# TensorE instead of VectorE for the transposes of couples 6 to 11, with natural rows, in an attention-plus-SiLU kernel

## The chip, the cores and the metric

The kernel runs on one core of a Trainium2 chip. The metric is the device time of one execution in microseconds (us). The engines are named as in the profile: PE (TensorE, matmuls), PEld (its weight loads), DVE (VectorE), ACT (ScalarE), POOL (GpSimd), SP (SyncE, which here only issues DMAs).

## The reference

Inputs: q, k, v of shape (8 batches, 12 heads, 448 tokens, 64), gains g_q and g_k of 64, w_in (768 x 2048), w_out (2048 x 768), all float32. Cut to what is computed:

```python
q_n = q / sqrt(mean(q*q, -1) + 1e-6) * g_q          # k_n likewise with g_k
scores = (1/8) * q_n @ k_n.T                        # per batch and head
attn = exp(scores - max); attn /= sum(attn) + 1e-9
x = (attn @ v)  -> (8*448, 12*64) = (3584, 768)     # heads side by side
h = x @ w_in
out = (h * sigmoid(h)) @ w_out                      # (3584, 768)
```

## The kernel before, in words

**Units of work.** A *couple* is two pairs of heads, that is four heads of one batch; a batch has three couples and the kernel NC = 24, counted here from 0. `GROUP` is 6: six couples are two batches. The outer loop is `for c in range(NC): visit(c); between(c)`. `visit(c)` is the attention of couple c: `scores` (L701, PE, with the exponentials in L706 on ACT) and `weigh` (L738, PE, the product with v) take turns, and `divide` (L796, DVE) multiplies the result of couple c-1 with the reciprocal row sums and puts it into xT. `between(c)` prepares couple c+1 and the norms of c+2, and runs the *filler*.

**The filler.** From couple 4 on, matmuls of the first dense layer for batches that are done stand between the visits. They come from a generator (`halves_in`, with `Seven`: a Strassen-Winograd scheme with seven products of three matmul steps, L870) that `fill(others, prompt)` steps on for a given number of columns. `others` are small pieces of work dealt out evenly over these steps; `prompt` are pieces dealt at the first step and then every third. Each product is written into one of two PSUM banks "mm", and taken out by ACT (L878, L888) or DVE (L828); POOL adds two intermediate sums (L890, L891). A finished block gets silu on ACT (L1008) and is stored to a DRAM tensor `hidden` by SP (`save`, L903) from one of three `stage` buffers, which is free for the next block when the store has landed. After the last couple, the second dense layer runs in seven quads (L1177, L1214), from 743 us to the end, and stores the output.

**Weights.** Pieces of w_in are fetched (L84), taken apart and rounded on ACT, DVE and POOL (L99, L100, L122 to L133) among the fill pieces until couple 9 or so, and their Strassen sums are formed on DVE (L825, L828).

**Norms and transposes.** Scores need q and k with the head dimension on the partitions. The root mean square of k is not applied to k: it is the scale of the exponentials (`norm.column`). That of q is multiplied into the rows of q by POOL. There are two ways:

- *Early way, couples 0 to 5.* Rows of q and k are loaded in natural rows of 256 bytes or more: 112 partitions with four neighbouring tokens each for q, 128 partitions with three each for k. `norm.squares_q` and `squares_k` square on ACT (L458) and reduce on DVE (L459); `norm.root` makes mean plus epsilon on DVE (L483) and the power -0.5 on POOL (L487); `norm.scale` multiplies q on POOL (L502). `transpose_q` (L620) and `transpose_k` (L636) transpose on PE against the identity `ident` into a PSUM tile "sc" (two buffers, shared with the scores), and ACT copies qT (L624) and kT with the gains (L638) out.
- *Late way, couples 6 to 23.* q is loaded in eight pieces of 128-byte runs (`load_quarters`, L249), k twice: plain, in six DMAs, for the norms (L276, L278), and in eight quarters for the transposes. `flip` transposes 32 x 32 blocks of q and of k on DVE (L644, L647), and `gain` multiplies kT with the gains on ACT (L653). The squares of q (`sum_squares`: L661 on ACT, L662 on DVE) then lie in halves on two partitions, so `scale(c)` adds them with two matmuls against `ident` (L673), after `pair_up` has changed `ident` for that (L686); the root follows on DVE (L674) and POOL (L677), the multiplication on POOL (L680). v comes in four DMAs (L303) and four for the rest (L314, L316), against one (L307) and three (L320, L323) in the early way.

Tokens of couples 0 to 5 (batches 0 and 1) thus lie permuted (token 4p + j at column 112 j + p), and `store` undoes this when it writes the output, in pieces that are cut at 112 rows. From batch 2 on (`plain=2`) the order is natural and pieces are cut at the end of a batch only.

**Order.** The order on each engine is the order in which the program issues, written out by hand. SP takes its DMAs in program order too, and waits at each for what it needs: a load that waits for a buffer holds up all that is behind it. In `between(c)` of the late way the order is: `flip` q of c+1 and the load of q for c+2 behind it; a first fill, with the key norms of c+2 among its others; `sum_up` (row sums of couple c, L772); a second fill, with the two halves of the reciprocals (L781, the second followed by `spread`, which moves them between partitions by six DMAs, L787 and L789), `flip` of k, `gain` and `sum_squares(c+2)` as prompt pieces; then `scale(c+2)`. For c = 5 the same pieces run without a fill between them, and the norms of couple 6 stand in visit 5.

Of the kernel before, what the change touches and what calls it, by code (L numbers as in the profile page):

```python
# [30 lines left out]
class Shapes:  # L31
    def __init__(self, q, w_in):
# [19 lines left out]
        assert self.NW == self.NPAIR and self.B % 2 == 0  # L52

        self.Q = 32
        assert 2 * self.S == self.NK and 4 * self.Q == self.P and self.D == 2 * self.Q
# [134 lines left out]
def kernel(  # L190
# [25 lines left out]
    nc = tc.nc  # L216
# [34 lines left out]
    def load_q(c, t, steps=1):  # L251


        b, cp = divmod(c, z.NPAIR // 2)
        rows = q[b, ts(cp, 4)]
        if c >= z.NPAIR:
            load_quarters(rows, t)
            return
        for i in range(steps):
            n = 4 // steps  # L260
            dst = t[0:R, ts(i, nq // steps)].rearrange("p (n j d) -> p n (j d)", n=n, j=J)
            nc.sync.dma_start(dst, rows[ts(i, n)].rearrange("n (p j) d -> p n (j d)", j=J))
# [5 lines left out]
    def load_k(c):  # L268
        t = place[f"k{c % 2}"]
        if c >= z.NPAIR:  # L270
            t = place["k0"]
            for i, start in enumerate((z.KA, z.KB)):
                main, left = plain(k, c, i)
                dst = t[:, ds(start, z.KL)].rearrange("p (j h d) -> p h j d", j=z.KEYS, h=2)
                for h in range(2):
                    nc.sync.dma_start(dst[:, h], main[:, h])  # L276
                dst = t[ds(i * z.LEFT, z.LEFT), ds(z.KL, 2 * D)]
                nc.sync.dma_start(dst.rearrange("p (h d) -> p h d", h=2), left)  # L278
            return
# [17 lines left out]
    def load_v(c):  # L297
        if c >= z.NPAIR:
            dst = place["v"].rearrange("p (i h j d) -> p i h j d", i=2, h=2, d=D)
# [9 lines left out]
    def load_v_rest(c):  # L309
        if c >= z.NPAIR:  # L310
            for i in range(2):
# [215 lines left out]
def bounded(  # L527
# [12 lines left out]
    )  # L540
    GROUP = z.NPAIR
    EARLY = GROUP - 1

# [67 lines left out]
    def transpose_q(c):  # L611
# [13 lines left out]
        if c == GROUP - 2:  # L625
            load_q(GROUP)

    def transpose_k(c):
# [9 lines left out]
        nc.scalar.activation(kT, columns, AF.Copy, scale=gains)  # L638
        loads["k" if c < GROUP - 1 else "quarters"](min(c + 2, GROUP))

# [159 lines left out]
    def normalise(c):  # L800


        def piece(name, i):
            if name == "q":
                norm.squares_q(c, raw_of(c), scratch[i], i)
                norm.root(c, name, i)
                norm.scale(c, raw_of(c), q_of(c), i, nc.gpsimd)
                if i == 1 and c + 2 < GROUP:
                    load_q(c + 2)
            else:  # L810
                late = c >= GROUP
                rows = place["k0" if late else f"k{c % 2}"]
                norm.squares_k(c, rows, scratch[0 if late else i], i)
                if i == 1:
                    norm.root(c, name)
                    if late and c + 1 < NC:
                        loads["k"](c + 1)

# [401 lines left out]
    def save_out(q, i, j):  # L1220
        for t in range(2):
            store(
                nc, out, z, (4 * q + 2 * (i - 1) + t) * P, results[i, j][t], (j - 1) * z.HALF,
                nc.gpsimd if q == QUADS - 1 and i == 2 else nc.sync, plain=2,
            )

    def quad(q):
# [53 lines left out]
        if q == QUADS - 1:  # L1281

            def then(t, h):
                store(
                    nc, out, z, (4 * q + t) * P, c[1, 2][t][:, ts(h, QUARTER)],
                    z.HALF + h * QUARTER, *((nc.scalar, nc.sync)[:: 1 if h else -1]), plain=2,
                )
# [75 lines left out]
    def visit(c):  # L1363

        if c < GROUP - 1:
            beside = normalise(c + 1)
        elif c == GROUP - 1:
            beside = [lambda: sum_squares(c + 1), lambda: scale(c + 1)] + normalise(c + 1)[2:]
        else:
            beside = []  # L1370
        if c < NC:
            scores(c, 0, 0)
        run_all(beside[0:1])
        if c > 0:
            weigh(c - 1, LEFT)
            weigh(c - 1, LEFT - 1, 0)
            turn(1, nc.scalar.copy if c < GROUP else nc.vector.tensor_copy)
        if c < NC:
# [47 lines left out]
    def between(c):  # L1426

        def transposes_and_sums():
            summing = sum_up(c)
            if c < GROUP:  # L1430
                next(summing)
            if c < GROUP - 1:
                transpose_k(c + 1)
            reciprocals = next(summing)
            if GROUP - 1 <= c < NC - 1:
                reciprocals += [lambda: flip(c + 1, "k"), gain]
# [3 lines left out]

        if c < GROUP - 1:
            transpose_q(c + 1)
# [272 lines left out]
```

## Time and profile before

| | us |
|---|---|
| median of three runs (1344.6 to 1344.99) | 1344.6 |
| the profiled execution, its own time | 1346.0 |
| its span, first to last instruction | 1344.1 |
| PE busy | 1300.4 |
| DVE busy | 951.8 |
| ACT busy | 502.3 |
| POOL busy | 369.5 |

The granted clock of PE over the span is 0.994 of full speed. "Busy" is the union of the instructions' times. A row of an instruction group reads: line, engine, operation, what is written and read, shapes, count, then busy time, the mean of one in ns, and the idle time of the engine just before them with what ended it. A row of the time order reads: start, duration, engine, line, operation, and in brackets the idle time before it and its releaser. Windows of the span are given in us from its start.

### The profile page before, as it was taken

What the parts mean: (1) busy time and instruction counts of PE and PEld (TensorE: products, weight loads), DVE (VectorE), ACT (ScalarE), POOL (GpSimd) and SP (SyncE); (2) the same over time, 40 slices, a digit from 0 to 9 for tenths busy, and PEclk for the clock granted to TensorE, in tenths of its full rate; (3) what the DMA queues carried; (4) which work ended last, traced back from release to release, by engine and by line L of the source; (5) the groups of instructions that cost most, each with busy time, mean ns of one, the idle gap of its engine ahead of it and who ended that gap; (6) DMA issues with size and microseconds to landing.
All of it is one profiled execution on the core that took longest, in us unless ns stands there. A gap on an engine that the chain in (4) does not pass through costs nothing.

```text
span 1344.1 us, 19812 instructions
## 1 busy us (share of the span) xinstructions
PE 1300.4 (97%) x7111; PEld 828.3 (62%) x7111; DVE 951.8 (71%) x1630; ACT 502.3 (37%) x877; POOL 369.5 (27%) x223
## 2 busy tenths in 40 slices
PE   8997998999999999999999999999999999999997
PEld 4332443444444444444444455557999999999997
DVE  5786876785855655855554586789978787878785
ACT  7874455556445545455544244420000000101000
POOL 5765344443343343343331044410000000000000
PEclk9998999999999999999999999999999999999999
DMA  8565456434433543443421257422323232332311
GB/s 230 155 147 123 119 155 161 106 89 109 108 91 88 124 93 87 124 97 86 112 74 38 101 176 262 149 98 71 103 75 99 75 102 77 99 100 79 125 48 39
DMA packets 286543, 147.69 MB, mean 110 GB/s; under 512 B 224420, under 2 KB 270372, under 8 KB 286436
## 3 DMA queue, kind: packets, MB, share of 16 engines
q1 hardware_dynamic: 285872, 145.35, 39.6%
q8 instruction: 58, 0.95, 0.3%
q0 software_dynamic: 256, 0.79, 0.2%
q14 instruction: 49, 0.40, 0.1%
q10 hardware_dynamic: 308, 0.20, 0.0%
HBM read 96.73 MB, written 41.29 MB: 103 GB/s over the span
## 4 chain that ended last, share of the span: by engine, by line
PE 81%; DVE 7%; ACT 4%; DMA 3%; issue 2%; SPq 2%; POOL 0%; ACTq 0%; DVEq 0%
PE mm L870 24%; PE alone L1177 22%; PE av L738 8%; PE sc L701 8%; PE mm L1177 7%; PE alone L870 7%; PE alone L1214 2%; DVE work L781 1%; DVE work L752 1%; DMA rows<-in_k_dram 1%; PE sc L772 1%; SPq L249 1%; DVE sums_x L825 1%; PE mm L1214 1%; ACT L1008 1%
## 5 line engine op out<-in xcount | busy, mean ns | idle before, releaser
L870 PE MATMUL mm<-x,W 128*128 128x448 f32 x636 | 258.6, 549 | 12.0 <-DVE parts L828 3.3
L706 ACT ACTIVATE work<-sc,rms 128x448 f32<-128x448 f32 x324 | 185.5, 635 | 86.2 <-PE sc L701 62.8
L870 PEld LDWEIGHTS mm<-x,W 128*128 128x128 f32 x636 | 117.6, 191 | 146.8 <-issue 114.7
L870 PE MATMUL mm<-sums_x,W 128*128 128x448 f32 x456 | 186.5, 548 | 6.8 <-DVE parts L828 4.8
L701 PE MATMUL sc<-work 64*64 64x448 f32 x1344 | 167.3, 550 | 1.7 <-DVE rms L674 1.1
L738 PE MATMUL av<-work,rows 64*64 64x448 f32 x1296 | 156.0, 546 | 4.7 <-ACT av L714 1.8
L752 DVE TENSOR_TENSOR work<-work 128x896 f32<-128x896 f32 (+1 forms) x114 | 123.7, 1115 | 49.4 <-PE av L738 48.8
L870 PEld LDWEIGHTS mm<-sums_x,W 128*128 128x128 f32 x456 | 85.1, 191 | 100.2 <-issue 83.4
L487 POOL TENSOR_TENSOR rms<-rms,minus_half 128x14 f32<-128x14 f32 (+3 forms) x37 | 88.3, 2389 | 134.6 <-DVE rms L483 133.9
L514 POOL DMA_DIRECT2D out_dram<-x x2 | 1.3, 652 | 443.0 <-DVE x L828 443.0
L1177 PE MATMUL alone<-W,rows 128*128 128x192 f32 x608 | 113.0, 326 | 0.0
L738 PEld LDWEIGHTS av<-work,rows 64*64 64x64 f32 x1296 | 60.7, 133 | 76.0 <-issue 35.4
L677 POOL TENSOR_TENSOR rms<-rms,minus_half 128x28 f32<-128x28 f32 x18 | 86.2, 4791 | 74.7 <-DVE rms L674 63.3
L1177 PEld LDWEIGHTS alone<-W,rows 128*128 128x128 f32 x608 | 101.2, 190 | 0.0
L701 PEld LDWEIGHTS sc<-work 64*64 64x64 f32 x1344 | 55.5, 134 | 69.1 <-ACT work L706 26.9
L890 POOL TENSOR_TENSOR parts<-parts,stage 128x448 f32<-128x448 f32 x31 | 42.0, 1355 | 150.3 <-DVE parts L828 149.9
L1177 PE MATMUL alone<-W,work 128*128 128x192 f32 x382 | 72.2, 326 | 0.0
L1008 ACT ACTIVATE stage<-stage 128x896 f32<-128x896 f32 x63 | 57.4, 947 | 24.7 <-DVE stage L828 24.1
L1177 PEld LDWEIGHTS alone<-W,work 128*128 128x128 f32 x382 | 63.8, 190 | 0.0
L1187 ACT COPY rows<-alone 128x192 f32<-128x192 f32 x34 | 10.9, 320 | 137.4 <-PE alone L1177 78.9
L781 DVE RECIPROCAL work<-sc 128x224 f32<-128x224 f32 x36 | 55.6, 1547 | 5.2 <-PE sc L772 5.0
L459 DVE TENSOR_REDUCE rms<-rows 128x8 f32<-128x512 f32 (+2 forms) x48 | 30.2, 629 | 40.3 <-ACT rows L458 37.5
(243 smaller groups left out, 2104.9 us busy)
## 6 DMA issues: line engine op xcount, KB each, us to landing
hidden<-stage SPq DMA_DIRECT2D x63, 448.0 KB, 3.1
work<-hidden SPq DMA_DIRECT2D x21, 1024.0 KB, 5.1
rows<-in_moe_w_out_dram SPq DMA_DIRECT2D x32, 384.0 KB, 3.4
W<-in_moe_w_in_dram SPq DMA_DIRECT2D x22, 512.0 KB, 5.0
work<-work SPq DMA_DIRECT2D x144, 56.0 KB, 2.0
rows<-in_q_dram SPq DMA_DIRECT2D x144, 56.0 KB, 2.3
rows<-in_k_dram SPq DMA_DIRECT2D x144, 56.0 KB, 2.4
x<-hidden SPq DMA_DIRECT2D x7, 1024.0 KB, 5.6
```

The costliest lines, as they stand in the source:

```text
L487: nc.gpsimd.tensor_tensor(out=t, in0=t, in1=half, op=ALU.pow)
L677: nc.gpsimd.tensor_tensor(out=f, in0=f, in1=minus_half.to_broadcast([P, n]), op=ALU.pow)
L701: nc.tensor.matmul(two[ds(half * D, D), h, 0:S], keys[rows, ts(half, D)], qT[rows, pair, :], start=True, stop=True,)
L706: nc.scalar.activation(eleft[:, h] if j == LEFT else weights(c, j)[:, i, h], two[:, h, 0:S], AF.Exp, scale=norm.column(c, i, h, j),)
L738: nc.tensor.matmul(sums[i][ds(h * D, D), :], v, w, start=(j == 0 and step == 1), stop=(j == LEFT - 1 and step == 1),)
L752: nc.vector.tensor_tensor(out=total, in0=total, in1=more, op=ALU.add)
L781: nc.vector.reciprocal(out=r[0][:, rows], in_=t[:, rows])
L870: nc.tensor.matmul(t, self.left(name, s), self.right(name, s), start=s == ends[0], stop=s == ends[1])
L890: nc.gpsimd.tensor_tensor(out=u2, in0=u2, in1=p5, op=ALU.add)
L1008: nc.scalar.activation(t, t, AF.Silu)
L1177: nc.tensor.matmul(t, x[:, i], y, start=i == ORDER[0], stop=i == ORDER[-1])
L1214: nc.tensor.matmul(o, a[:, 2 * i + m, t], right_one(name, i)[:, m], start=n == 0, stop=n == len(steps) - 1,)
```

## The change

A constant `LATE` = 12 takes the place of `GROUP` = 6 as the couple from which the late way is used. Couples 6 to 11 go the early way for loads, norms and transposes, with these differences from couples 0 to 5: q is loaded by two DMAs straight into the place where it is scaled, in the order j, h, d (256-byte runs); one root serves both halves of q, followed by two scales in place; the norms of q for couple c+2 are dealt as others of the second fill (for couples 6 and 7 they stand in visits 5 and 6). `pair_up`, the first `sum_squares` and the first `scale` of the late way move to `between(10)`. Tokens of batches 2 and 3 are permuted too, so the output of four batches is stored in the cut pieces (`plain=4`).

```diff
+        self.LATE = 2 * self.NPAIR
 def load_q(c, t, steps=1):
+        if c >= z.LATE:
+            load_quarters(rows, t)
+            return
         if c >= z.NPAIR:
-            load_quarters(rows, t)
+            for i in range(2):
+                dst = t[0:R, ts(i, nq // 2)].rearrange("p (j h d) -> p j h d", j=J, h=2)
+                nc.sync.dma_start(dst, rows[ts(i, 2)].rearrange("h (p j) d -> p j h d", j=J))
             return
 def load_k(c):  # the same in load_v and load_v_rest
-        if c >= z.NPAIR:
+        if c >= z.LATE:
 def transpose_q(c):
         if c == GROUP - 2:
             load_q(GROUP)
+        elif c >= GROUP:
+            load_q(c + 1)
 def transpose_k(c):
-        loads["k" if c < GROUP - 1 else "quarters"](min(c + 2, GROUP))
+        loads["k" if c < LATE - 1 else "quarters"](min(c + 2, LATE))
 def normalise(c):
         def piece(name, i):
+            t = scratch[i if c < GROUP + 2 else 0]
+            source = raw_of(c) if c < GROUP else q_of(c)
             if name == "q":
-                norm.squares_q(c, raw_of(c), scratch[i], i)
+                norm.squares_q(c, source, t, i)
+            else:
+                norm.squares_k(c, place["k0" if c >= LATE else f"k{c % 2}"], t, i)
+            if name == "q" and c < GROUP:
                 norm.root(c, name, i)
-                norm.scale(c, raw_of(c), q_of(c), i, nc.gpsimd)
+                norm.scale(c, source, q_of(c), i, nc.gpsimd)
...
+            elif i == 1:
+                norm.root(c, name)
+                if name == "q":
+                    for m in range(2):
+                        norm.scale(c, source, q_of(c), m, nc.gpsimd)
+                elif LATE <= c < NC - 1:
+                    loads["k"](c + 1)
 def save_out(q, i, j):  # and in the last quad
-                nc.gpsimd if q == QUADS - 1 and i == 2 else nc.sync, plain=2,
+                nc.gpsimd if q == QUADS - 1 and i == 2 else nc.sync, plain=4,
 def visit(c):
-        if c < GROUP - 1:
-            beside = normalise(c + 1)
-        elif c == GROUP - 1:
-            beside = [lambda: sum_squares(c + 1), lambda: scale(c + 1)] + normalise(c + 1)[2:]
-        else:
-            beside = []
+        beside = normalise(c + 1) if c <= GROUP else []
 def between(c):
-            if c < GROUP - 1:
+            if c < LATE - 1:
                 transpose_k(c + 1)
             reciprocals = next(summing)
-            if GROUP - 1 <= c < NC - 1:
+            if LATE - 1 <= c < NC - 1:
                 reciprocals += [lambda: flip(c + 1, "k"), gain]
...
-        if c < GROUP - 1:
+        if c < LATE - 1:
             transpose_q(c + 1)
         elif c < NC - 1:
             flip(c + 1, "q")
...
-        further = normalise(c + 2)[2:] if c >= GROUP - 1 else []
-        queries = [lambda: sum_squares(c + 2)] if c >= GROUP - 1 else []
-        fill(late + weights_in(c, 0) + further)
+        further = normalise(c + 2) if c >= GROUP - 1 else []
+        fill(late + weights_in(c, 0) + further[2:])
...
-        fill(weights_in(c, 1), prompt[:3] + [lambda: run_all(prompt[3:] + queries)])
-        if c == GROUP - 2:
-            pair_up()
+        if c >= LATE - 2:
+            if c == LATE - 2:
+                prompt.append(pair_up)
+            queries = prompt[3:] + [lambda: sum_squares(c + 2)]
+            fill(weights_in(c, 1), prompt[:3] + [lambda: run_all(queries)])
+        else:
+            fill(weights_in(c, 1) + (further[:2] if c >= GROUP else []), prompt)
...
-        if c >= GROUP - 1:
+        if c >= LATE - 2:
             scale(c + 2)
```

More of the change, by code (lines that the diff above doesn't have):

```diff
@@ L297, in load_v @@
     def load_v(c):
-        if c >= z.NPAIR:
+        if c >= z.LATE:
             dst = place["v"].rearrange("p (i h j d) -> p i h j d", i=2, h=2, d=D)
@@ L309, in load_v_rest @@
     def load_v_rest(c):
-        if c >= z.NPAIR:
+        if c >= z.LATE:
             for i in range(2):
@@ L540, in bounded @@
     )
-    GROUP = z.NPAIR
+    GROUP, LATE = z.NPAIR, z.LATE
     EARLY = GROUP - 1
@@ L803, in piece @@
         def piece(name, i):
+            t = scratch[i if c < GROUP + 2 else 0]
+            source = raw_of(c) if c < GROUP else q_of(c)
             if name == "q":
-                norm.squares_q(c, raw_of(c), scratch[i], i)
+                norm.squares_q(c, source, t, i)
+            else:
+                norm.squares_k(c, place["k0" if c >= LATE else f"k{c % 2}"], t, i)
+            if name == "q" and c < GROUP:
                 norm.root(c, name, i)
-                norm.scale(c, raw_of(c), q_of(c), i, nc.gpsimd)
+                norm.scale(c, source, q_of(c), i, nc.gpsimd)
                 if i == 1 and c + 2 < GROUP:
                     load_q(c + 2)
-            else:
[L811 to L817, printed above, removed]
+            elif i == 1:
[5 more added lines that the diff above has]
+                    loads["k"](c + 1)
         if c >= NC:
@@ L1285, in then @@
                     nc, out, z, (4 * q + t) * P, c[1, 2][t][:, ts(h, QUARTER)],
-                    z.HALF + h * QUARTER, *((nc.scalar, nc.sync)[:: 1 if h else -1]), plain=2,
+                    z.HALF + h * QUARTER, *((nc.scalar, nc.sync)[:: 1 if h else -1]), plain=4,
                 )
@@ L1363, in visit @@
     def visit(c):
-        if c < GROUP - 1:
-            beside = normalise(c + 1)
-        elif c == GROUP - 1:
-            beside = [lambda: sum_squares(c + 1), lambda: scale(c + 1)] + normalise(c + 1)[2:]
-        else:
-            beside = []
+        beside = normalise(c + 1) if c <= GROUP else []
         if c < NC:
@@ L1376, in visit @@
             weigh(c - 1, LEFT - 1, 0)
-            turn(1, nc.scalar.copy if c < GROUP else nc.vector.tensor_copy)
+            turn(1, nc.scalar.copy if c <= GROUP else nc.vector.tensor_copy)
         if c < NC:
```

## The prediction, made before the changed kernel was run

> **What bounds the kernel now.** I read the page's busy shares first, then cut the span into couples (a couple's visit begins with its first scores matmul, L701) with the table by stage, then read the order of time in the couples that the change touches.
>
> ```profile
> PE 1300.4 (97%) x7111; PEld 828.3 (62%) x7111; DVE 951.8 (71%) x1630; ACT 502.3 (37%) x877; POOL 369.5 (27%) x223
> ...
> 103.40:131.40 28.00, 21.26 (x153) 7.68 (x152) 19.53 (x26) 15.42 (x28) 16.08 (x10) 0.90 0.50 108
> 131.40:168.90 37.50, 35.04 (x179) 15.60 (x178) 30.06 (x45) 17.91 (x29) 15.28 (x9) 0.93 0.49 118
> 168.90:203.40 34.50, 32.90 (x178) 14.89 (x177) 26.71 (x36) 20.09 (x33) 16.60 (x9) 1.00 0.60 152
> 203.40:243.40 40.00, 34.40 (x175) 15.63 (x174) 27.17 (x35) 20.53 (x34) 16.71 (x9) 0.96 0.55 144
> 243.40:276.80 33.40, 32.59 (x175) 15.02 (x174) 27.96 (x35) 20.21 (x33) 15.20 (x8) 1.00 0.44 105
> 276.80:313.10 36.30, 32.79 (x176) 15.10 (x176) 29.34 (x35) 18.95 (x31) 16.45 (x8) 1.00 0.44 111
> ```
>
> The first line is the whole kernel: PE bounds it. The rest are couples 5 to 10 (counted from 0), one line each: window, its length, busy time of PE, PEld, DVE, ACT and POOL, then granted clock. Length less PE busy is PE's idle time: 6.7, 2.5, 1.6, 5.6, 0.8 and 3.5 us. Couples 13 to 21, which do the same with VectorE's transposes but without the rounding of w_in, have at most 0.4 us each. So just the couples where the change works leave PE 14 us idle (6 to 10), after 6.7 in couple 5, and only they run at a granted clock below 1. Two places carry it. The end of couple 5, in order of time (start, duration, engine, line; in brackets the idle time before and who ended it):
>
> ```profile
> 122.76 4.12 PE L870 MATMUL mm<-x,W 128*128 128x448 f32 x6 [2.38 <-DVE work L781]
> 130.80 0.62 PE L673 MATMUL sc<-rms,ident 128*128 128x28 f32 x2 [3.92 <-DVE rms L662]
> 131.36 1.77 PE L701 MATMUL sc<-work 64*64 64x448 f32 x8
> ...
> 168.85 0.98 PE L701 MATMUL sc<-work 64*64 64x448 f32 x8
> ```
>
> PE waits 2.4 us for the reciprocals (L781), then about 4 us for the sums of squares of couple 7's queries (L662); the eight matmuls after it take 1.77 us instead of 0.98, which is the halved clock. And couple 8:
>
> ```profile
> 219.65 2.31 SPq L303 DMA_DIRECT2D rows<-in_v_dram  x4
> 222.05 4.07 SPq L249 DMA_DIRECT2D rows<-in_q_dram  x8
> 226.22 0.90 SPq L903 DMA_DIRECT2D hidden<-stage  x2
> 229.50 0.53 ACT L888 COPY stage<-mm 128x448 f32<-128x448 f32 x1 [8.56 <-DMA hidden<-stage]
> 230.08 2.52 PE L870 MATMUL mm<-x,W 128*128 128x448 f32 x6 [2.55 <-ACT stage L888]
> 234.62 4.22 PE L870 MATMUL mm<-sums_x,W 128*128 128x448 f32 x6 [2.02 <-DVE parts L828]
> ```
>
> The silu rows were ready at 219.8, but their save stands on SP behind four v loads and eight q loads; the stage buffer comes free at 229.5, ACT sits 8.6 us, PE runs out of banks twice, and the clock drops again (0.96).
>
> [...] slow matmuls run from 122.8 to 126 and from about 130 to 136 us, after 2.4 and 3.9 us of idling. [...] the trace has 273 ns (L636) and 259 ns (L620), but groups of eight pass in 0.8 to 0.9 us because they overlap, and couples 1 to 4, which use them, keep a clock of 1.00. [...] one subtraction of L825 took 1.73 us beside the scale on POOL (L680), 0.62 otherwise.
>
> **The change part by part.** Prices are the rows of before:
>
> ```profile
> L677 POOL TENSOR_TENSOR rms<-rms,minus_half 128x28 f32<-128x28 f32 x18 | 86.2, 4791 | 74.7 <-DVE rms L674 63.3 <-DVE av L714 9.3 <-DMA rows<-in_k_dram 2.2
> L680 POOL TENSOR_TENSOR rows<-rows,rms 128x896 f32<-128x896 f32 x18 | 32.3, 1796 | 1.4
> L644 DVE STREAM_TRANSPOSE work<-rows 128x896 f32<-128x896 f32 x18 | 19.8, 1102 | 0.0
> L662 DVE TENSOR_REDUCE rms<-rows 128x28 f32<-128x896 f32 x18 | 19.5, 1086 | 22.8 <-ACT rows L661 21.6 <-ACT av L714 1.1
> L624 ACT COPY work<-sc 128x896 f32<-128x896 f32 x5 | 4.5, 908 | 0.0
> ```
>
> 1. *PE, added, on the path.* Eight q and seven k transposes for each of couples 6 to 11, in couples 5 to 10. In couples 3 and 4 the q group held PE 0.82 and 0.92 us (73.30 to 74.22, 93.52 to 94.34), the k group 0.91. About 1.78 us, six times: **+10.7**. The k group's wait for its score bank (0.46 and 0.73 us there) stays out: it now follows a whole fill. Nor does the q group idle there.
> 2. *PE, removed.* Six pairs of L673 at 0.30: **-1.8**. The waits before them: about 4.1 in couple 5 (28.00 less 21.26 less the 2.4 for L781) and 0.5 in couple 9: **-4.6**. What is late next: couple 6's first scores need only the copied qT and kT and the key roots, all done by about 119; divide of couple 5 needs the spread of the reciprocals, and SP issues that at once instead of after eight q loads (119.2 to 124.0). The 2.4 us for L781 stays: the bank is held by the same two reciprocals.
> 3. *Clock.* Couples 5 and 6 lose 0.10 x 28 + 0.07 x 37.5 = 5.4 us. The second stretch, some 6.8 us at half speed, follows the L673 wait and goes: **-3.4**. The first stays. Bounds: 0 to -5.4.
> 4. *SP.* A couple's loads fall from 30 DMAs (q 8, k 6 + 8, v 4 + 4) to 10 (2, 4, 1 + 3). At 0.48 us (median of L249) to 0.6 that is about 9 us of queue less per couple. In couple 8, from 217.1 on, v's rest, v and q take about 3.6 us instead of 9: the save is issued near 221, its buffer is free near 224, before PE wanted the bank (227.5). Of 5.6 us idle I keep 0.8: **-4.8**, and its clock loss, 0.04 x 40: **-1.6**. Bounds: 0 to -7.2.
> 5. *DVE.* Per couple -1.10 - 1.07 (the block transposes) - 1.09 - 0.19, + two reduces at 0.68 + 0.35: -1.7 us. It pays only where PE waits for DVE: couples 7 and 10: **-0.6** and **-1.2**, bounds 0 and -5. Couple 6 gets it the other way: the squares of couple 7 now stand in visit 6 ahead of the twelve operations of sum_x, which end just when the fill begins (145.9 against 144.8): 0.9 us of DVE, and its scale then blocks sum_x: **+1.0**, bounds -2 to +2.5. That scale ends some 0.5 us before the transposes of q 7 want it; if late, PE waits, and behind it the whole fill.
> 6. *ACT*: one copy of 0.91 and 0.3 of squares more per couple; gain (1.04) becomes the copy of kT. It ran 20 of 34 us, so 0; without that cover 0.9 us ahead of an eviction in each of six couples. In return ACT no longer sits in gain waiting for the key flip (4.7 and 5.1 us in couples 7 and 8), with evictions behind it.
> 7. *POOL*: 4.79 + 1.70 go; a root of 16 columns comes (2.58 for 14, 4.79 for 28: about 2.9) and two scales at 1.04. Less by 1.5, at the fill's end or in the visit, where no L890 waits: 0.
> 8. *Moved to couples 10 and 11*: the pairing of ident (four copies at 0.2 us on POOL), 16 quarter loads and the first L673; couples 13 to 21 show these hidden in steady state: 0, at worst +1.
> 9. *Stores.* Batches 2 and 3 are cut at 112 rows too: six more pieces in each column half, 12 DMAs on an SP that mostly waits for results: 0.
>
> Sum: 10.7 - 1.8 - 4.6 - 3.4 - 4.8 - 1.6 - 0.6 - 1.2 + 1.0 = **-6.3** against the profiled run's 1346.0 (span 1344.1 and 1.9 around it). The median of the runs is 1.4 lower, 1344.6, so the forecast is 1338.3.
>
> **The rivals.** *More gain*: no clock drop at all (another 2 us) and DVE's relief takes most idle time of couples 6, 7 and 10: -12, 1332.6. For it: all those waits name DVE. Against: PE then meets ACT and the reciprocals. *Wash*: the 2.4 us wait still triggers the clock drop for its full length (+2 to 3.4) and couple 8 is half cured (+3): about -0.5, 1344.1. *Slower*, by one mechanism: idle time re-forms behind the transposes. PE pays 10.7 and saves 6.4 certainly; if the save of couple 8 is still late (SP stands until 216.5 behind a w_in load that waits for POOL, whatever the other loads cost) and the clock falls as before, nothing else comes back, and couple 6 adds its 1.0: +5.3, 1349.9. It decides once ACT's wait at L888 in couple 8 stays over about 6 us. Against it: of the queue after 217.1, two thirds are loads that go. The diff leaves no room for the change not doing what it says.
>
> **How the numbers follow.** Chances: forecast 0.60, more gain 0.17, wash 0.14, slower 0.09. 0.2% is 2.7 us, about what a measurement of this kernel can tell from no change. Faster takes the first two whole but for 0.03, and 0.04 of the wash: 0.78; within, 0.13; slower, 0.09. The range goes from the larger gain to just past the wash: 1332 to 1346.
>
> **What would show it.** Right: no L673 before couple 10, a clock of 1 in couple 8, no ACT wait of over 3 us on hidden<-stage, couples 5 to 10 together 209.7 - 6 = some 203 us, couples from 12 on as before. Wrong: PE idle over 2 us in couple 8, a clock under 0.93 in couples 5 or 6, or the transposes waiting for POOL.

## The result and the profile after

The changed kernel takes **1333.36 us** (median of 6 runs, 1331.46 to 1335.99) against 1344.2 (6 runs, 1342.48 to 1344.99): ratio 0.9921, 95% interval 0.9908 to 0.9935. That is 10.8 us less, where 6.3 less was forecast. The profiled execution took 1333.6 us. The diff adds lines, so L701 is now L709, L738 L746, L870 L882, L673 L681, L781 L789, L828 L840, L888 L900, L878 L890 and L903 L915.

The first view is the page, busy time by engine; the next the table by stage with the same columns as before (window, length, busy time of PE, PEld, DVE, ACT and POOL, granted clock), one line for each of couples 5 to 10.

```profile
PE 1301.7 (98%) x7189; PEld 833.1 (63%) x7189; DVE 942.2 (71%) x1623; ACT 506.6 (38%) x890; POOL 363.8 (27%) x229
```

```profile
103.40:123.60 20.20, 19.24 (x164) 7.77 (x163) 14.12 (x19) 14.80 (x29) 10.99 (x5) 1.00 0.40 98
123.60:162.20 38.60, 36.08 (x190) 16.65 (x189) 32.71 (x51) 21.55 (x36) 19.28 (x12) 0.96 0.39 105
162.20:196.40 34.20, 33.58 (x188) 16.34 (x188) 24.31 (x34) 19.97 (x35) 14.55 (x10) 1.00 0.46 135
196.40:231.50 35.10, 34.00 (x189) 16.17 (x189) 24.88 (x35) 21.14 (x35) 15.79 (x10) 1.00 0.55 152
231.50:264.80 33.30, 33.30 (x188) 16.41 (x187) 24.91 (x32) 21.21 (x36) 13.30 (x8) 1.00 0.34 94
264.80:301.50 36.70, 34.56 (x194) 15.54 (x193) 29.62 (x35) 19.76 (x31) 17.33 (x13) 1.00 0.41 106
```

PE is as busy as before, with 78 more instructions, while the span fell from 1344.1 to 1331.8. The six couples take 198.1 us together instead of 209.7, which is 11.6 of the 12.3; the work after the last couple takes 600.5 instead of 601.1, so the cut stores cost nothing. Couple 5 is 7.8 us shorter, couple 8 is 5.0 shorter, and of these six only couple 6 has a clock below 1.

The end of couple 5 in order of time:

```profile
119.63 2.97 DVE L789 RECIPROCAL work<-mm 128x224 f32<-128x224 f32 x2 [2.16 <-PE mm L780]
120.53 0.53 ACT L890 COPY stage<-mm 128x448 f32<-128x448 f32 x1 [1.58 <-PE mm L882]
121.11 2.52 PE L882 MATMUL mm<-x,W 128*128 128x448 f32 x6 [0.62 <-ACT stage L890]
123.56 0.98 PE L709 MATMUL sc<-work 64*64 64x448 f32 x8
```

There is no L681 and no 4 us wait any more, and the 2.38 us for the reciprocals are gone too: PE waits 0.62 us for an eviction by ACT (a copy that takes a product out of its bank), and the first scores of couple 6 follow at full speed. The reciprocals themselves (L789) run until 122.60, but the fill's last product starts at 121.11: it does not wait for their bank, as there are two. Couple 8, in order of time:

```profile
205.33 3.50 SPq L85 DMA_DIRECT2D W<-in_moe_w_in_dram  x2
...
211.27 0.54 SPq L313 DMA_DIRECT2D rows<-in_v_dram  x1
211.92 1.91 SPq L263 DMA_DIRECT2D rows<-in_q_dram  x2
213.92 1.62 SPq L915 DMA_DIRECT2D hidden<-stage  x2
...
219.00 0.53 ACT L900 COPY stage<-mm 128x448 f32<-128x448 f32 x1 [4.31 <-PE sc L644]
```

One v DMA and two q DMAs stand where four and eight stood. ACT's eviction L900 now ends its idle time on PE's own transposes (L644), not on the landing of `hidden`, and couple 8 keeps a clock of 1.00.

### The profile page after: what moved, and what is told of

It is laid out like the page before. It is cut to its first block, busy times and chain, and to the rows that moved or that the text cites. A ratio compares the mean times of both kernels' runs of the same rounds, so it can differ in the third digit from the quotient of the medians.

```text
span 1331.8 us, 19793 instructions
## 1 busy us (share of the span) xinstructions
PE 1301.7 (98%) x7189; PEld 833.1 (63%) x7189; DVE 942.2 (71%) x1623; ACT 506.6 (38%) x890; POOL 363.8 (27%) x229
## 4 chain that ended last, share of the span: by engine, by line
PE 84%; DVE 7%; ACT 3%; issue 3%; DMA 2%; POOL 1%; SPq 0%; ACTq 0%; DVEq 0%; POOLq 0%
PE mm L882 26%; PE alone L1189 22%; PE av L746 8%; PE sc L709 7%; PE mm L1189 7%; PE alone L882 7%; PE alone L1226 2%; DVE work L760 1%; PE sc L780 1%; DVE work L789 1%; DVE sums_x L837 1%; DMA work<-work 1%; PE mm L1226 1%; PE sc L644 1%; PE sc L626 0%
## 5 line engine op out<-in xcount | busy, mean ns | idle before, releaser
L882 PE MATMUL mm<-x,W 128*128 128x448 f32 x636 | 256.7, 546 | 6.1 <-DVE parts L840 2.3
L714 ACT ACTIVATE work<-sc,rms 128x448 f32<-128x448 f32 x324 | 184.7, 633 | 81.0 <-PE sc L709 64.9
L882 PEld LDWEIGHTS mm<-x,W 128*128 128x128 f32 x636 | 116.7, 190 | 138.0 <-issue 109.0
L882 PE MATMUL mm<-sums_x,W 128*128 128x448 f32 x456 | 183.7, 543 | 1.6 <-DVE parts L840 1.6
L709 PE MATMUL sc<-work 64*64 64x448 f32 x1344 | 168.2, 549 | 2.6 <-ACT work L714 1.4
L746 PE MATMUL av<-work,rows 64*64 64x448 f32 x1296 | 156.6, 543 | 6.3 <-ACT av L722 1.8
L493 POOL TENSOR_TENSOR rms<-rms,minus_half 128x14 f32<-128x14 f32 (+4 forms) x43 | 106.4, 2476 | 149.8 <-DVE rms L489 140.2
L882 PEld LDWEIGHTS mm<-sums_x,W 128*128 128x128 f32 x456 | 85.1, 190 | 90.7 <-issue 82.8
L746 PEld LDWEIGHTS av<-work,rows 64*64 64x64 f32 x1296 | 59.9, 133 | 78.0 <-issue 35.5
L709 PEld LDWEIGHTS sc<-work 64*64 64x64 f32 x1344 | 55.2, 134 | 73.8 <-ACT work L714 27.6
L685 POOL TENSOR_TENSOR rms<-rms,minus_half 128x28 f32<-128x28 f32 x12 | 57.5, 4794 | 67.2 <-DVE rms L682 58.0
L465 DVE TENSOR_REDUCE rms<-rows 128x8 f32<-128x512 f32 (+2 forms) x56 | 35.9, 641 | 42.5 <-ACT rows L464 38.9
L1199 ACT COPY rows<-alone 128x192 f32<-128x192 f32 x34 | 10.8, 317 | 137.8 <-PE alone L1189 79.0
L789 DVE RECIPROCAL work<-sc 128x224 f32<-128x224 f32 x36 | 55.7, 1548 | 5.2 <-PE sc L780 5.0
```

What stands on the lines that cost most here:

```text
L493: nc.gpsimd.tensor_tensor(out=t, in0=t, in1=half, op=ALU.pow)
L685: nc.gpsimd.tensor_tensor(out=f, in0=f, in1=minus_half.to_broadcast([P, n]), op=ALU.pow)
L709: nc.tensor.matmul(two[ds(half * D, D), h, 0:S], keys[rows, ts(half, D)], qT[rows, pair, :], start=True, stop=True,)
L714: nc.scalar.activation(eleft[:, h] if j == LEFT else weights(c, j)[:, i, h], two[:, h, 0:S], AF.Exp, scale=norm.column(c, i, h, j),)
L746: nc.tensor.matmul(sums[i][ds(h * D, D), :], v, w, start=(j == 0 and step == 1), stop=(j == LEFT - 1 and step == 1),)
L789: nc.vector.reciprocal(out=r[0][:, rows], in_=t[:, rows])
```

## The experiments

Ratios are to the kernel before, run on the same chip. "Before" and "after" in the headings say on which kernel the edit was made. Differences to after are of medians taken on different chips, on which the medians of before lie between 1343.4 and 1344.4 us. Lengths of couples are of one profiled run of each kernel.

**1. The save on ACT's queue (b_save_act, on before).**

```diff
-        nc.sync.dma_start(hidden[f, :, ds(column, t.shape[1])], t)
+        queue = nc.scalar if column == 0 else nc.sync
+        queue.dma_start(hidden[f, :, ds(column, t.shape[1])], t)
```

> The kernel before, with the stores to hidden of the first two batches (couples 6 to 11) issued from ACT instead of SP. Queue theory (in couple 8 the store stood behind v and q loads on SP): ACT's wait on hidden<-stage in couple 8 falls from 8.6 to under 4 us, PE's idle time there from 5.6 to under 2 us, the couple's clock loss of 1.6 us goes: 1344.2 - 5 = about 1339, the other couples as before. Rival (couple 8 was held by VectorE's and ACT's chains, the queue is incidental): idle time of couple 8 stays above 4 us, total within 1.5 us of before, or slower by ACT's issue time.

Measured: 1344.59 against 1343.61, ratio 1.0002 (0.9995 to 1.0010). Couple 8 fell from 40.04 to 36.21 us with a clock of 1.00. The order of time in it:

```profile
224.46 0.33 ACTq L904 DMA_DIRECT2D hidden<-stage  x1
...
225.81 0.38 ACTq L904 DMA_DIRECT2D hidden<-stage  x1
...
227.54 0.53 ACT L888 COPY stage<-mm 128x448 f32<-128x448 f32 x1
228.12 0.30 PEld L870 LDWEIGHTS mm<-x,W 128*128 128x128 f32 x2 [0.52 <-ACT stage L888]
```

The eviction L888 has no wait for `hidden` in front of it. So most of couple 8's loss was the save standing in SP's queue. But couples 7, 9 and 11 became 1.07, 1.16 and 1.14 us longer, with more PE idle before L870 and L673. Two of the expected numbers missed: PE is still idle for 3.5 us in couple 8, not under 2, and the total did not fall, since what is gained in couple 8 is lost in the other three. How the save on ACT makes them longer was not followed further.

**2. The loads cut up again (a_split, on after).** The natural loads of couples 6 to 11 move the same bytes in 30 DMAs a couple, as many as the late way has; PE's transposes stay.

```diff
-                nc.sync.dma_start(dst, rows[ts(i, 2)].rearrange("h (p j) d -> p j h d", j=J))
+                src = rows[ts(i, 2)].rearrange("h (p j) d -> p j h d", j=J)
+                for j in range(J):
+                    nc.sync.dma_start(dst[:, j], src[:, j])
...
+                for j in range(z.KEYS):
+                    for h in range(2):
+                        nc.sync.dma_start(dst[:, j, h], src[:, j, h])
...
+            for n in range(4):
+                nc.sync.dma_start(dst[:, n], main[:, n, 0 : z.KEYS - 1])
```

> The changed kernel, with the q, k and v loads of couples 6 to 11 cut into as many DMAs as before (8, 14 and 8 a couple, same bytes and layout). Queue theory: the store of couple 8 is late again, its idle time goes back from 1.1 to 3 us or more, and couples 5 to 10 lose 3 to 7 us: 1336.5 to 1340.5. Rival (the gain came from VectorE's and ACT's relief): idle time of couple 8 under 2 us, total within 1.5 us of 1333.4.

Measured: 1346.29, ratio 1.0020 (1.0013 to 1.0027): 13 us slower than after, and slower than before. Couple 8 is back at 39.64, while couples 5, 7, 9 and 10 stay within 0.1 us of after. Couple 8 and the middle of couple 6 in order of time:

```profile
222.36 5.26 SPq L265 DMA_DIRECT2D rows<-in_q_dram  x8
227.71 0.88 SPq L931 DMA_DIRECT2D hidden<-stage  x2
230.48 0.53 ACT L916 COPY stage<-mm 128x448 f32<-128x448 f32 x1 [7.55 <-DMA hidden<-stage]
231.06 2.52 PE L898 MATMUL mm<-x,W 128*128 128x448 f32 x6 [2.07 <-ACT stage L916]
```

```profile
128.17 4.17 SPq L297 DMA_DIRECT2D rows<-in_k_dram  x6
132.43 2.48 SPq L811 DMA_DIRECT2D work<-work  x4
138.41 1.21 DVE L820 TENSOR_TENSOR x<-av,work 128x448 f32<-128x448 f32 x2 [6.70 <-DMA work<-work]
139.09 2.34 PE L762 MATMUL av<-work,rows 64*64 64x448 f32 x8 [6.41 <-DVE x L820]
```

The save again follows eight q DMAs, ACT again waits 7.6 us. A second victim shows: the spread of the reciprocals (L811) follows 14 k DMAs, `divide` (L820) waits, and PE waits 6.4 us behind it. Couples 4 and 6 lose 4.6 us each in this way, two thirds of the 13. The number of DMAs is thus a sufficient cause of couple 8's loss; its 14 k DMAs ahead of the spread are harsher than the order before, so the losses of couples 4 and 6 are no measure of what before lost there.

**3. The change ended at couple 9 (a_late9 and a_late9_k, on after).** The last three couples go back to the late way.

```diff
-        self.LATE = 2 * self.NPAIR
+        self.LATE = 9
...
-                nc.gpsimd if q == QUADS - 1 and i == 2 else nc.sync, plain=4,
+                nc.gpsimd if q == QUADS - 1 and i == 2 else nc.sync, plain=3,
```

> The kernel after with the change ended at couple 9 instead of 12 (LATE = 9): couples 6, 7 and 8 go the early way, 9 to 11 the late way again, token order natural from batch 3 on. Theory (the gain of couple 8 is SP's queue, the gain of couples 5 and 6 is what the first couples need): couples 5 and 6 stay at 20.2 and 37 to 39 us, couple 8 has 30 loads again before the save and goes back to 38.5 to 40 (35.1 after), couples 9 and 10 change by less than 0.7 each, as they did between before and after; total 3 to 5 us above after, 1336.5 to 1338.5. Rival (PE transposes cost about 1 us per couple wherever they stand, and couple 8's wait was of the w_in load ahead of it, not of the loads): three couples give back 3 us and couple 8 stays near 35, total 1330 to 1331.

Measured: 1347.77, ratio 1.0033 (1.0021 to 1.0045), far over both forecasts. The key transposes of couple 8 (L644, in couple 7) waited 5.17 us for a load of key rows, whose cause the next expectation tells; with the clock loss (0.92) couple 7 took 41.2 us. The second kernel exchanges the two buffers:

```diff
-            load_quarters(k[b, ts(cp, 4)], place["k1"])
+            load_quarters(k[b, ts(cp, 4)], place["k0"])
...
-            t = place["k0"]
+            t = place["k1"]
...
-        nc.vector.transpose(kT, place["k1"])
+        nc.vector.transpose(kT, place["k0"])
```

> As a_late9, with the two key buffers of the late way exchanged. In a_late9 the rows of couple 9's keys were loaded over those of couple 8 before these were transposed (so couple 8's keys were not the reference's there), and TensorE waited 5.3 us for that load in couple 7, with half a clock behind it; here the load goes into the other buffer. Theory (couple 8's gain is the SP queue): couple 7 falls from 41.2 to 34 to 35 us; couple 8 stays at 38.5 to 40, as in before, couples 9 and 10 at 33.4 and 36.3; total 3 to 6 us above after, 1336.5 to 1339.5. Rival (couple 8 was late only because couple 7 was disturbed, and the wait is of the w_in load ahead of the queue): couple 8 near 35, total 1331 to 1333.

Measured: 1338.84 against 1344.35, ratio 0.9959 (0.9945 to 0.9973), 5.5 us over after. Couple 7 fell to 34.85; couples 5 and 6 keep their gain (20.16 and 38.62); couples 9 and 10 have before's lengths (33.42, 36.26); couple 8 takes 39.67. In order of time:

```profile
211.62 2.18 SPq L309 DMA_DIRECT2D rows<-in_v_dram  x4
...
213.89 4.21 SPq L250 DMA_DIRECT2D rows<-in_q_dram  x8
...
218.20 0.90 SPq L915 DMA_DIRECT2D hidden<-stage  x2
...
220.99 0.53 ACT L900 COPY stage<-mm 128x448 f32<-128x448 f32 x1 [8.06 <-DMA hidden<-stage]
```

This is the picture of before (8.56 us of waiting there). So the first three couples bring half of the change's gain, through couples 5 and 6, and the last three the other half, in couple 8, where the queue of before is back and, with it, the flips on DVE.

**4. The change carried to couple 17 (a_late18, on after).** `LATE = 3 * NPAIR`, `plain=6`.

> The changed kernel with LATE = 18 (and plain = 6 in the stores): couples 12 to 17 also take the transposes on PE. In the windows of couples 12 to 16 PE is idle 0.6 us at most, so nothing can be won back. Theory (the transposes cost PE 1.68 us a couple on the path, less 0.30 for L673, and only relieved queues pay for them): couples 11 to 16 grow by 1.38 us each, less 0.6 idle once: +7 to +8.5, total 1340.5 to 1342. Rival (transposes on PE are cheaper than VectorE's in themselves): no change or faster than 1333.4.

Measured: 1339.43, ratio 0.9971 (0.9960 to 0.9982), 6.1 us over after. Couples 12 to 17 take 35.54, 35.04, 35.09, 34.82, 34.96 and 34.53 us, against 34.30, 34.09, 34.13, 33.54, 34.11 and 34.13 in after: 1.24, 0.95, 0.95, 1.29, 0.85 and 0.40 more. Couple 11 takes 0.69 more, couple 10 1.11 less. PE's transposes for couples 12 to 17 stand in couples 11 to 16, which are 1.0 us longer on average. That is their bare price, less what goes with the late way, where no wait is there to be removed: somewhat less than the 1.38 expected.

**5. VectorE's work put back (a_vector, on after).** Two reduces of 128x896, 1.09 us each, stand where the block transposes stood, in the same six couples.

```diff
+    def load_vector(t):
+        nc.vector.tensor_reduce(
+            out=unused, in_=t.rearrange("p (n e) -> p n e", e=z.Q), axis=AX.X, op=ALU.add
+        )
...
+                reciprocals += [lambda: load_vector(qT.rearrange("p i s -> p (i s)"))]
...
+                load_vector(kT)
```

> The changed kernel, with two VectorE reduces over 128x896 (1.09 us each, into a tile that nothing reads) for each of couples 6 to 11 where the two block transposes were. It costs VectorE what they cost, without the loads, without gain on ACT waiting for it. VectorE theory: PE's idle time in couples 6 to 10 (6.4 us) rises by 3 us or more, total 1336 to 1339. Rival (relief of VectorE was worth little, the waits were SP's and ACT's): under 1.5 us more, total within 1.5 us of 1333.4.

Measured: 1337.43, ratio 0.9953 (0.9940 to 0.9966), 4.1 over after. In the profiled run couples 5 to 10 are 2.8 us longer: couple 6 by 0.6, 8 by 1.1, 10 by 1.0, the others by at most 0.1. PE's idle time in couples 6 to 10 rose from 6.4 to 10.1 us, as the VectorE theory has it. More than half of that, 2.0 us, is in couple 6, which grew less because its clock stays at 1.00 here. The rest of the 4.1 includes a stretch at half clock at 751 us, far from the edit.

**6. Gain later (b_gain_later, on before).** In couple 5, the key flip and the gain come after the second fill.

```diff
-            run_all(transposes_and_sums())
+            held = transposes_and_sums()
+            run_all(held[:2])
...
+        if c == GROUP - 1:
+            run_all(held[2:])
```

> The kernel before, with the block transpose of the keys and gain of couple 6 (end of couple 5) issued after the second fill instead of before the first. Theory: the 2.4 us that PE waited for the reciprocals (L781) and part of the 4.1 us before L673 came from gain, which stood on ACT ahead of the copy that frees the other bank: the wait falls to about 0.6 us, the one before L673 to 1 to 2 us, and with them one or both halved-clock stretches: couples 5 and 6 together 65.5 - 4 to 7 us, total 1338 to 1341. Rival (the prediction's reading: the bank is held by the reciprocals themselves): the 2.4 us stay, and the total is within 1.5 us of before.

Measured: 1343.17, ratio 0.9999 (0.9991 to 1.0007). In before, DVE and ACT stood so:

```profile
119.66 2.96 DVE L781 RECIPROCAL work<-mm 128x224 f32<-128x224 f32 x2
...
123.62 1.05 ACT L653 ACTIVATE work<-work,gains 128x896 f32<-128x896 f32 x1 [5.71 <-DVE work L647]
...
124.57 0.51 ACT L878 COPY stage<-mm 128x448 f32<-128x448 f32 x1
```

and with the edit:

```profile
118.27 2.96 DVE L781 RECIPROCAL work<-mm 128x224 f32<-128x224 f32 x2
119.03 0.53 ACT L878 COPY stage<-mm 128x448 f32<-128x448 f32 x1 [2.50 <-PE mm L870]
...
119.62 2.52 PE L870 MATMUL mm<-x,W 128*128 128x448 f32 x6 [0.62 <-ACT stage L878]
...
126.74 0.38 PE L673 MATMUL sc<-rms,ident 128*128 128x28 f32 x2 [4.60 <-DVE rms L662]
...
129.70 1.04 ACT L653 ACTIVATE work<-work,gains 128x896 f32<-128x896 f32 x1 [3.12 <-DVE work L647]
...
130.79 1.77 PE L701 MATMUL sc<-work 64*64 64x448 f32 x8 [3.68 <-ACT work L653]
```

The 2.38 us wait is gone, though the reciprocals take as long as before. In before the last product of the fill (the six matmuls of L870) starts at 122.76, right behind L781 (119.66 to 122.62) and 1.8 us ahead of the eviction L878: it is written into the bank that the reciprocals read, so their release was the real one. The other bank was worse off: ACT sat in gain (L653) 5.7 us for the key flip, with its eviction L878 behind it. With the edit L878 comes early, and the product starts right behind it, at 119.62, while L781 runs until 121.23: it is written into the other bank. So what the edit changed is which bank the product takes, and with it whom it waits for. All fourteen profiles agree: the product waits for DVE where gain is issued between the reciprocals and the fill (before and experiments 1, 7 and b_norm_turn in 8) or the keys' copy on ACT behind the row sums (experiment 10), and for ACT in all others. How the banks are dealt out stays open.

Yet couples 5 and 6 together only fell from 65.5 to 64.4, since L673 still waits 4.6 us and the scores now wait for the gain.

**7. The norms of couple 7 moved one visit on (b_norm_visit6, on before)**, as the change does for them, without PE's transposes.

```diff
+        elif c == GROUP:
+            beside = [lambda: sum_squares(c + 1), lambda: scale(c + 1)]
...
-        queries = [lambda: sum_squares(c + 2)] if c >= GROUP - 1 else []
+        queries = [lambda: sum_squares(c + 2)] if c >= GROUP else []
...
-        if c >= GROUP - 1:
+        if c >= GROUP:
             scale(c + 2)
```

> The kernel before, with sum_squares and scale of couple 7 moved from the end of couple 5 into visit 6 (as those of couple 6 stand in visit 5); transposes and loads stay as they were. Theory: of the 7.8 us that couple 5 lost under the change, 4.1 are the wait before L673 and it takes the second halved-clock stretch with it: couples 5 and 6 together 65.5 - 5 to 7 us, total 1336.5 to 1339. Rival (the next wait takes its place, gain on ACT or the spread of the reciprocals in visit 6): couples 5 and 6 fall by under 2.5 us, total 1341 or more.

Measured: 1341.9, ratio 0.9986 (0.9980 to 0.9993). Couple 5 fell to 21.83, but couple 6 rose to 42.76 at a clock of 0.88, together 64.6 against 65.5, so the rival held:

```profile
131.02 1.77 PE L738 MATMUL av<-work,rows 64*64 64x448 f32 x8 [3.84 <-DVE av L714]
```

The wait of about 4 us went with the norms: L714 (of before), the `turn` copy on DVE, now stands behind the sums of squares (L662). The diff changes the line of that copy as well (`nc.scalar.copy if c <= GROUP`), which neither the cut diff above nor the sum has.

**8. The same with the turn on ACT (b_norm_turn), and with the key flip ahead of the reciprocals too (b_flip_first), both on before.**

```diff
-            turn(1, nc.scalar.copy if c < GROUP else nc.vector.tensor_copy)
+            turn(1, nc.scalar.copy if c <= GROUP else nc.vector.tensor_copy)
```

```diff
-            run_all(transposes_and_sums())
+            pieces = transposes_and_sums()
+            run_all(pieces[2:] + pieces[:2])
```

> The kernel before, transposes and loads untouched, with three edits of order: sum_squares and scale of couple 7 in visit 6 (as in b_norm_visit6), the one-column copy of turn in visit 6 on ACT, and at the end of couple 5 the key flip and gain ahead of the reciprocals. Theory (couple 5 was held by a chain through two in-order queues: reciprocals, flip, gain, and behind gain on ACT the evictions and all squares): with gain done some 3 us earlier ACT has no backlog in visit 6, and couples 5 and 6 together fall from 65.5 to 59.5 to 62.5 us, total 1337 to 1340.5. Rival (only taking the flips, or the 16 quarter loads, away helps; the reciprocals, now 1 us later, and their spread become the wait): couples 5 and 6 at 63.5 or more, total 1341 or more.

> As b_flip_first but with the key flip and gain where they were, behind the reciprocals. Theory (gain on ACT is the root): ACT's backlog stays, the copy of turn on ACT comes about 1 us earlier than on VectorE, no more: couples 5 and 6 at 63 to 65 us, total 1340 to 1342. Rival (the copy of turn behind VectorE's queue was the whole wait of 3.8 us in visit 6): couples 5 and 6 at 58 to 61 us, total 1335.5 to 1338.5.

Measured: b_norm_turn 1340.21, ratio 0.9974 (0.9963 to 0.9985), couples 5 and 6 together 61.2; b_flip_first 1340.26, ratio 0.9975 (0.9966 to 0.9983), together 62.6. With the turn on ACT the wait in visit 6 is 1.05 instead of 3.84:

```profile
130.19 0.98 PE L738 MATMUL av<-work,rows 64*64 64x448 f32 x8 [1.05 <-ACT av L714]
```

Moving the norms together with the turn thus brings 3 to 4 of the 6.7 us that couples 5 and 6 gain. Where the flip stands makes no difference in the time of the whole: my theory for b_norm_turn, that it would keep most of the loss, missed in the couples (they came out between theory and rival), though the total lies within the theory's range. In both kernels couple 8 is shorter too (37.9 and 38.8 us), which no edit here touches; in the five profiles that keep before's loads and saves it takes 37.9 to 40.0, so a single couple 8 is known to some 2 us.

**9. The turn back on VectorE (a_turn_vector, on after)**, the reverse line.

> The changed kernel with the one-column copy of turn in visit 6 back on VectorE, where it stands behind the first reduce of couple 7's queries. Theory (a small line of the change that the prediction left out pays its way): PE waits 1.5 to 2.5 us more for the copy, but the wait for the spread behind it shrinks by as much: couple 6 within 1 us, total 1332.5 to 1334.5. Rival (the waits add, and the clock falls for another stretch): couple 6 up by 2 to 4 us, total 1335.5 to 1337.5.

Measured: 1334.6, ratio 0.9934 (0.9920 to 0.9947), 1.2 over after and not to be told from it. Couple 6 takes 38.28: PE waits 1.44 us for the copy in place of the spread. In the changed kernel the line matters little, perhaps (not tested) since the squares are reduced there in pieces of 0.7 us (L465) instead of one of 1.1 (L662).

**10. The spread earlier (a_spread, on after).** In couple 5 half of the first four spread DMAs go to ACT's queue, and the key transposes follow the row sums.

```diff
-                    nc.sync.dma_start(mine[1][i, h], mine[0][1, h])
+                    queue = nc.scalar if c == GROUP - 1 and h else nc.sync
+                    queue.dma_start(mine[1][i, h], mine[0][1, h])
...
-            if c < LATE - 1:
+            if c < LATE - 1 and c != GROUP - 1:
                 transpose_k(c + 1)
...
+            if c == GROUP - 1:
+                transpose_k(c + 1)
```

> The changed kernel, in couple 5 alone: the key transposes of couple 6 behind the row sums instead of between their parts, and the first four DMAs of the spread on two queues (SP and ACT). Theory: the 1.8 us that PE waited in visit 6 for divide, which waited for the spread's DMAs, go, and with them the halved clock of 3.4 us there: 1333.4 - 1.8 - 1.7 = 1330 to 1331.5. Rival (the wait moves on to sum_x and the row sums of couple 6, where VectorE is full): within 1 us of 1333.4.

It aims at what is late next in the changed kernel, in couple 6:

```profile
127.61 1.14 SPq L797 DMA_DIRECT2D work<-work  x2
130.21 1.21 DVE L804 TENSOR_TENSOR x<-av,work 128x448 f32<-128x448 f32 x2 [2.09 <-DMA work<-work]
130.89 1.18 PE L746 MATMUL av<-work,rows 64*64 64x448 f32 x6 [1.81 <-DVE x L804]
```

Measured: 1332.33, ratio 0.9919 (0.9906 to 0.9932). The wait for L804 went and couple 6 keeps its clock, but smaller waits came up (1.57 us for L789 in couple 5, where the last product takes the reciprocals' bank again, and 1.1 in two waits for evictions by DVE in couple 6); the two couples take 58.0 instead of 58.8. It is the lowest median here, 1.0 below after, which these runs can't tell apart.

## Why the prediction was right, and where it was off

The direction, the places and the two mechanisms were right; the gain was 4.5 us larger than forecast, nearest to the rival "more gain" (12 us less; but one stretch at half clock remains, and only part of the surplus is DVE's relief). By couple, the forecast's own terms (six times 1.78; L673 goes twice from couple 5 and once each from 6 to 9) against the traces, in us:

| couples | forecast | measured (profiled after less before) |
|---|---|---|
| 5 and 6 | 3.56 - 0.9 - 4.1 - 3.4 + 1.0 = -3.8 | 58.8 - 65.5 = -6.7 |
| 7 | 1.78 - 0.3 - 0.6 = +0.9 | -0.3 |
| 8 | 1.78 - 0.3 - 4.8 - 1.6 = -4.9 | -5.0 |
| 9 | 1.78 - 0.3 - 0.5 = +1.0 | -0.1 |
| 10 | 1.78 - 1.2 = +0.6 | +0.4 |

1. *PE's transposes* were sized well: a q group holds PE 0.82 us, a k group 0.86, together 1.68 against 1.78. In this profile they waited for POOL 0.34 us, in couple 5; but in a_late9 and a_late18, where couple 6 keeps its clock and PE comes sooner, those of q 7 wait 0.78 us for POOL's scale, the risk that item 5 named. Alone, in experiment 4, the transposes cost about 1 us net a couple, where the sum has 1.78 less 0.30.
2. *The wait for L673* went as forecast. *"The 2.4 us for L781 stays: the bank is held by the same two reciprocals"* **is the step that failed**. The reciprocals hold their bank as long as before, until 122.60, but the product no longer goes there: it takes the other bank and waits 0.62 us for ACT's eviction. In before that eviction stood behind gain. Item 6 priced the going of gain at nothing, although it named its waits in couples 7 and 8. Experiment 6 shows that moving flip and gain is enough for this; which of the two it takes, it doesn't show.
3. *Clock.* The first stretch, which the sum kept (122.6 to 126.1 us, granted clock 0.50), went with that wait. Another came in couple 6 (132.3 to 135.7 us, again 0.50), after the 1.8 us wait for the spread. That couple is 1.1 us longer, almost the forecast's 1.0, but by the spread's late DMAs, not by the squares of couple 7 on DVE (experiment 10 leaves the squares and takes it to 37.2, below before's 37.5): the size was right for the wrong reason. The scale of couple 7 did slow sum_x, as item 5 had it: two of the twelve operations (L837) took 1.47 and 1.46 us beside it on POOL (L508, 135.58 to 138.49), the others 0.62. The slow stretch itself costs little of it: with the clock at 1.00 the couple takes 38.3 us in a_late9 and 38.1 in a_late18, against 38.6. But for one at the kernel's end, the stretches at 0.50 are 3.4, 6.8 and 3.4 us long in before (from 122.64, 129.47 and 235.28) and 3.4 us in after (from 132.29).
4. *SP.* Forecast 6.4 us with the clock, less the transposes. Three edits bear the mechanism out, but at a smaller size: a_split takes 4.55 of couple 8 back, a_late9_k 4.58 (with the flips back and PE's transposes gone from it), and b_save_act takes 3.8 from it without any other part of the change. DVE's relief, put at nothing in this couple, adds 1.1 (a_vector), and the transposes cost 0.5 less net than the sum has. So it is partly luck that couple 8 came out at -5.0 where -4.9 was forecast. The rival "slower" (the w_in load decides) is ruled out: that load still holds SP for 3.5 us, and the couple is cured.
5. *DVE's relief* was forecast at 1.8 in couples 7 and 10; a_vector makes it 2.8 in couples 6, 8 and 10 and nothing in 7. The sum fits roughly, the places only in couple 10; in couple 6 the relief is a gain of 0.6 where a loss of 1.0 was put down.
6. *Couples 7 and 9* came out 1.2 and 1.1 us better than forecast. PE's order of time shows where, from the start of one run of matmuls to the start of the next: the fill's last three took 5.22, 3.06 and 0.85 us in couple 7 before and take 4.61, 2.25 and 0.84 after; in couple 9 the first fell from 5.15 to 4.53 and the last, with the wait for L673 that was forecast, from 4.47 to 3.85. Before, PE waited in them for evictions by DVE (L828), 0.44 and 0.54 us in couple 7 and 0.27 in couple 9, and lost 0.2 to 0.4 us more at each, as runs that follow without a wait overlap (by 0.17 us in after, where one starts at 193.30 and the last ends at 193.47). On DVE the first of these evictions stands right behind the key flip, the second behind squares (L662) that ACT's gain had held up, the third right behind the query flip. But a_vector puts as much DVE work into the flips' places and leaves both couples unchanged, so that work alone isn't the cause. PE's own transposes now stand ahead of these runs and give DVE 0.8 us each time, and gain is gone: which of the two it is was not tested.
7. *The turn line* of the diff was not priced. It is worth 2.8 us of PE's waiting where the norms move without the rest (3.84 against 1.05), and nothing measurable in the changed kernel.

Two figures of the prediction's reading are off, by at most 0.3 us: 28.00 less 21.26 less 2.4 is 4.3, not 4.1, and couple 18 leaves PE 0.6 us idle, not at most 0.4.

What stays open: of the 6.7 us of couples 5 and 6, norms and turn bring 3 to 4; the remaining 2 to 4 go with flips, gain and quarter loads, which were not separated further. Medians of kernels that differ by under some 2 us were not told apart here, since a stretch at half clock (granted 0.50, so up to 1.7 us lost in 3.4 us, an estimate) can also fall far from the edit: at 751 us in a_vector, while before and after have a clock of 1.00 from 745 to 762 us.

## What to carry to other kernels

When a wait ends with the release of one of two banks, ask what the *other* bank was waiting for before you call the wait fixed: an instruction that sits in its engine's order waiting for a third one (here gain, for the flip) held up the eviction behind it, and without it the product took that other bank, 1.8 us sooner. Count DMAs, not bytes, on an in-order queue, and look for the small urgent ones (a save, a spread) behind bulk loads: 20 more DMAs a couple cost 13 us here with the same bytes. And pay for a slower unit only where a wait goes: the same change gave 5.5 us in couples 6 to 8, another 5.5 in couples 9 to 11, and cost 6.1 in couples 12 to 17.

## What was not expected of the hardware

A save issued from ACT took 0.33 and 0.38 us for its two DMAs in couple 8 of b_save_act, as long as one from SP in before (0.38, median of 63), yet three couples became 1.07 to 1.16 us longer.

In after, the half clock came back in couple 6 (0.50 from 132.29 to 135.70 us) behind a wait of only 1.8 us, while single waits of 0.5 to 1.1 us in couples 8 and 10 (2.1 us in all in couple 10) left it at 1.00. Nor does the idle time of a whole couple decide it: couple 10 keeps a clock of 1.00 in before with 3.5 us idle, couple 6 has 0.96 in after with 2.5. What does was not shown. And lost clock need not be lost time: couple 10, the late way in both, takes 36.3 us in before at a clock of 1.00 and in a_late9_k at 0.95, where PE waits 1.4 us less for the others.
